# Layer weights cast on the way in by GpSimd's DMAs, eight `zT` buffers, and five more q turned by the crossbar

## The chip, the cores and the metric

The kernel runs on one core of one Trainium2 chip. The metric is the time of one execution on the device in microseconds (us); less is better. Engines are named as in the profile: PE is TensorE's matrix multiplication (PEld its weight loads), DVE is VectorE, ACT is ScalarE, POOL is GpSimd, SP is SyncE, whose queue issues nearly all DMAs.

## The reference, cut to what matters

Attention with a threshold (8 batches, 8 heads, 576 positions, 64 wide), then a layer with a tanh-shrink on the joined heads (4608 tokens, 512 to 2048 to 512). All in float32.

```python
scores = scale * np.matmul(q, k.transpose(0, 1, 3, 2))
thresh = np.max(scores, axis=-1, keepdims=True) - tau
scores = np.where(scores >= thresh, scores, -1000000000.0)
scores = scores - np.max(scores, axis=-1, keepdims=True)
attn = np.exp(scores)
attn = attn / (np.sum(attn, axis=-1, keepdims=True) + 1e-09)
attn_out = np.matmul(attn, v)
x = attn_out.transpose(0, 2, 1, 3).reshape(B * S, H * D)
h = x @ w_in
g = h - np.tanh(h)
out = g @ w_out
```

## The kernel before, in words

The work is 32 pairs of heads, four pairs to a batch. A pair's 1152 score rows make nine tiles of 128 rows, so there are 288 tiles in all. One Python loop over `s` (line 663) writes out the order of all engines by hand: each turn of it is a *slot*, and in slot `s` tile `s + 8` gets its scores, tile `s + 5` its threshold, tile `s` its exponentials, and tile `s - 2` is multiplied with the values. Each engine runs its instructions in the order in which the loop wrote them, and waits for others by semaphores.

What happens to a tile: PE multiplies q with k in two halves (`psS`, lines 303 and 313; q and k are split into a high and a low fp16 part, which lie beside each other in the partitions, and `kS` is k's turned tile with its two halves of partitions swapped). DVE takes the scores out of PSUM with their row maximum (`sc`, line 323) and makes the shift from it (`nb`, line 337). ACT makes the threshold with a steep Prelu (`z`, line 357). The tile is turned, by PE (`psZ`, line 377) for pairs 0 to 3 and part of pairs 4 to 7, else by a crossbar DMA that SP issues (`zT`, line 365). ACT takes the exponentials (`pT`, lines 386 and 394), PE multiplies with the values (`psO`, lines 412 and 423), DVE divides by the sums (`osb`, lines 438 and 443) and, after one more turn on PE, copies the result into the layer's input (`xT`, `xR`).

The inputs of a pair are prepared some slots ahead by a plan (`PREP`, line 621). Where `first` is nine times the pair's number less 8, less 16, 15 and 14 slots from there SP loads k, q and v as float32. In slots `first - 8` and `first - 7` POOL splits k and q, each in three instructions (lines 176, 179, 180; tiles `khl` and `qhl`). In slot `first - 5` PE turns k with nine matrix products, DVE copies it out of PSUM (`kT`, line 250) and POOL copies the swapped halves (`kS`, line 256, two instructions). In slot `first - 4` POOL casts v (lines 208 to 213). q is turned like k in slot `first - 3` (line 227, copied out by DVE at line 250), or, where `q_by_dma(p)` holds, by one crossbar DMA in slot `first - 5` that SP issues and that writes `qT` directly (line 239). The pair's first scores stand in slot `first`.

The layer's work begins in slot 40 for the first stage, and is spread between the attention tiles: PE makes `psH` (line 478), ACT the tanh (`th`, line 491), DVE the difference (`g`, line 497), and PE the second product (`psY`, line 504), one batch behind. After the last tile the rest of the layer runs alone. The product with w_out begins with the second stage, in slot 76.

The layer's weights are two float32 matrices of 4 MB each. `w_pieces` (line 593) cuts each into eight pieces of 128x1024. In every fourth slot, from slot -5 on (`w_when`, line 651), SP loads the next piece into one of two buffers (`wt`, lines 613 and 617), after POOL has cast the piece loaded four slots earlier to bf16 (line 605). `w_load` and `w_cast` hold these two steps:

```python
if s + AHEAD in w_when:
    if loaded:
        w_cast()
    piece = next(pieces, None)
    if piece:
        w_load(piece)
```

Of the kernel before, what the change touches and what calls it, by code (L numbers as in the profile page):

```python
# [9 lines left out]
F32 = mybir.dt.float32  # L10
# [8 lines left out]
def kernel(  # L19
# [11 lines left out]
    nc = tc.nc  # L31
    P = 128
# [13 lines left out]
    HPAIR = H // 2  # L46
# [14 lines left out]
    AHEAD = 8  # L61
# [33 lines left out]
    for i in range(NM):  # L95
# [9 lines left out]
    pool = lambda name, bufs, **kw: ctx.enter_context(  # L105
        tc.tile_pool(name=name, bufs=bufs, **kw)
    )
# [4 lines left out]
    sc_pool = pool("sc", AHEAD - MASK + 2)  # L112
    st_pool = pool("st", 12)
    z_pool = pool("z", 4)
    zt_pool = pool("zt", 6)
    p_pool = pool("p", 3)
    o_pool = pool("o", 2)
    wt_pool = pool("wt", 2)
    g_pool = pool("g", 2)
    t_pool = pool("t", 3)  # L120
    y_pool = pool("y", 2)
# [108 lines left out]

    def q_by_dma(p):

        return p >= 2 * HPAIR and p % 2 == 1

    def turn(p, t):
        hl = hls.pop((p, t))
# [22 lines left out]
    def turn_first(t, part):  # L259

        hl = hls[0, t[0]]
        c0, c1 = ((0, 5), (5, TPP))[part]
        pl, tag = (ps_y, "y") if t == "ks" else (ps_h, "h")
        ps = pl.tile([P, 5 * P], FP16, name=f"ps1_{t}", tag=tag)
        for c in range(c0, c1):
            o = ps[:, (c - c0) * P : (c - c0 + 1) * P]
            if t == "ks":
                for a in range(2):
                    turn_chunk(o[64 * a : 64 * a + 64, :], c, hl[:, c, 1 - a, :])
            else:  # L270
                turn_chunk(o, c, hl[:, c, :, :].rearrange("p a d -> p (a d)"))
        if part == 0:
            mats[0, t] = qk_pool.tile([P, W], FP16, name=f"{t}T", tag=t)
        dst, n = mats[0, t][:, c0 * P : c1 * P], (c1 - c0) * P
        if part == 1 or t == "q":
            nc.scalar.copy(out=dst, in_=ps[:, 0:n])
        else:
            nc.vector.tensor_copy(out=dst, in_=ps[:, 0:n])
# [10 lines left out]
    def scores(i):  # L289
        p, j = divmod(i, TPP)  # L290
        qT, kT, kS = mats[p, "q"], mats[p, "k"], mats[p, "ks"]
        ps = ps_big.tile([P, 1024], F32, name="psS", tag="big")
        main, rem, lo = slice(0, 512), slice(512, 576), 0
        if kind(j) == "B":
            main, rem, lo = slice(512, 1024), slice(448, 512), 448
        if j == 4:
            qrem = REM
            if q_by_dma(p):
                qrem = (slice(512, 640, 2), slice(513, 640, 2))
            for n, kk in enumerate((kT, kS)):  # L300
                for dst, srcs in ((main, MAIN), (rem, REM)):
                    for hh in range(2):
                        nc.tensor.matmul(  # L303
                            out=ps[64 * hh : 64 * hh + 64, dst],
                            lhsT=qT[:, qrem[hh]], rhs=kk[:, srcs[hh]],
                            start=(n == 0), stop=(n == 1),
                        )
        else:
            hh = int(j > 4)
            lhs = qT[:, j * P : (j + 1) * P]  # L310
            for n, kk in enumerate((kT, kS)):
                for dst, src in ((main, MAIN[hh]), (rem, REM[hh])):
                    nc.tensor.matmul(  # L313
                        out=ps[:, dst], lhsT=lhs, rhs=kk[:, src],
                        start=(n == 0), stop=(n == 1),
                    )
        sc = sc_pool.tile([P, S], F32, name="sc")
        if kind(j) == "B":
            mx = mxs[i] = mxs.pop(i - 1)
        else:  # L320
            mx = mxs[i] = st_pool.tile([P, 2], F32, name="mx", tag="mx")
        c = int(kind(j) == "B")
        nc.vector.tensor_scalar(  # L323
            out=sc, in0=ps[:, lo : lo + S], scalar1=SC, scalar2=None,
            op0=ALU.mult, op1=ALU.max, accum_out=mx[:, c : c + 1],
        )
        scs[i] = sc

    def shift(i):

        kd = kind(i % TPP)
        if kd == "A":
            return
        n = 2 if kd == "B" else 1
        mx = mxs.pop(i)
        nb = st_pool.tile([P, 2], F32, name="nb", tag="nb")
        nc.vector.tensor_scalar(  # L337
            out=nb[:, 0:n], in0=mx[:, 0:n], scalar1=-1.0, scalar2=tau,
            op0=ALU.mult, op1=ALU.add,
        )  # L340
        nbs[i] = nb[:, n - 1 : n]
        if kd == "B":
            nbs[i - 1] = nb[:, 0:1]

    def kink(i):
        sc, nb = scs.pop(i), nbs.pop(i)
        kd = kind(i % TPP)
        if kd == "B":
            zt = zs.pop(i - 1)
            z = zt[:, S:W]  # L350
        elif kd == "A":
            zt = zs[i] = z_pool.tile([P, W], BF16, name="z")
            z = zt[:, 0:S]
        else:
            zt = zms[i // TPP % NM]
            z = zt[:, 0:S]
        nc.scalar.activation(  # L357
            out=z, in_=sc, func=ACT.Prelu, bias=nb, scale=1.0, alpha=STEEP
        )
        if on_pe(i):  # L360
            zts[i] = zt
        elif kd != "A":
            n = 5 if kd == "M" else TPP
            zts[i] = zt_pool.tile([P, TPP, P], BF16, name="zT")
            nc.sync.dma_start_transpose(out=zts[i][:, 0:n, :], in_=zt)
# [226 lines left out]

    def w_pieces():
        for w, sb, n in ((moe_w_in, w_in_sb, DM_C), (moe_w_out, w_out_sb, DF_C)):
            flat = sb.rearrange("p c n -> p (c n)")
            cols = n * w.shape[1] // 8
            src = w.rearrange("(c p) n -> p c n", p=P)
            for i in range(8):
                yield flat, src, i, cols, w.shape[1]

    loaded = []

    def w_cast():
        flat, wt, i, cols = loaded.pop(0)
        nc.gpsimd.tensor_copy(out=flat[:, i * cols : (i + 1) * cols], in_=wt)

    def w_load(piece):
        flat, src, i, cols, width = piece
        wt = wt_pool.tile([P, cols], F32, name="wt", tag="wt")
        if cols >= width:  # L610
            r = cols // width
            s = src[:, i * r : (i + 1) * r, :]
            nc.sync.dma_start(out=wt.rearrange("p (c n) -> p c n", n=width), in_=s)
        else:
            r = width // cols
            s = src[:, i // r, (i % r) * cols : (i % r + 1) * cols]
            nc.sync.dma_start(out=wt, in_=s)
        loaded.append((flat, wt, i, cols))


    PREP = (
# [26 lines left out]
    for t in ("k", "q", "v"):  # L648
        load(1, t)
    pieces = w_pieces()  # L650
    w_when = [4 * i + 3 for i in range(17)]

    todo, stage = [], 0
    fold = const.tile([P, 64], BF16, name="fold")
# [8 lines left out]
    for s in range(-AHEAD, NTILE + LAG + 3):  # L663
        p, j = divmod(max(s, 0), TPP)
        if 0 <= s < NTILE and j == 2 + LAG and p % HPAIR == 0 and p >= HPAIR:
            assert not todo
            todo = layers(stage, False)
            share = len(todo) / (HPAIR * TPP - 2 - LAG)
            done, stage = 0.0, stage + 1
        if 0 <= s + AHEAD - 1 < NTILE:  # L670
            shift(s + AHEAD - 1)
        if 0 <= s + AHEAD < NTILE:
            scores(s + AHEAD)
        if s == 1 - AHEAD:
            for t in ("k", "q", "ks"):
                turn_first(t, 1)
        for i in kinks.pop(s, []):
            kink(i)
        bend()
        if 0 <= s < NTILE:  # L680
            weights(s)
            if todo:
                done += share
                if j == TPP - 1 and p % HPAIR == HPAIR - 1:
                    done = 1e9
                while todo and done >= 1:
                    todo.pop(0)()
                    done -= 1
        if s == 0:
            nc.vector.tensor_tensor(  # L690
                out=fold, in0=ident_bf[:, 0:64], in1=ident_bf[:, 64:P], op=ALU.add
            )
        shrink()
        for store in stores[:-1]:
            store()
        del stores[:-1]
        if 0 <= s - LAG < NTILE:
            attend(s - LAG)
            pp, jj = divmod(s - LAG, TPP)
            if jj == 4:  # L700
                norm(pp, 0)
            if jj == 8:
                norm(pp, 1)
        pp, jj = divmod(s - LAG, TPP)
        if jj == 1 and 0 < pp <= NPAIR:
            emit_x(pp - 1)
        for step in plan.pop(s, []):
            step()
        if True:
            if s + AHEAD in w_when:  # L710
                if loaded:
                    w_cast()
                piece = next(pieces, None)
                if piece:
                    w_load(piece)

    while stage < NMB:
        for step in layers(stage, True):
# [44 lines left out]
```

## Time and profile before

| | |
|---|---|
| median of 6 runs | 544.73 us (544.27 to 545.67) |
| profiled execution, its own time | 544.8 us |
| its span in the profile | 542.7 us |
| PE busy | 509.5 us (94%), x4790 |
| DVE busy | 447.3 us (82%), x1196 |
| ACT busy | 439.4 us (81%), x630 |
| POOL busy | 291.0 us (54%), x390 |
| SP's DMA queue, share of 16 engines | 73.6% |
| HBM read, written | 36.70 MB, 9.44 MB |

The shares are means over stages that differ: the attention runs alone at first (to some 70 us), then attention and layer together (to some 470 us), then the layer alone. PE's clock was granted in full throughout. The part of the profiled execution's time that its span does not cover is 2.1 us.

### The profile page before, as it was taken

To read this page: it belongs to the slowest core of one execution; us is meant where nothing else is said; L and a number is where in the kernel's file an instruction comes from. 1 tells how busy PE (TensorE), PEld (TensorE's weight loads), DVE (VectorE), ACT (ScalarE), POOL (GpSimd) and SP (SyncE) were. 2 spreads that over 40 slices of the span, in tenths; PEclk is the share of its full clock that TensorE was granted. 3 is DMA by queue.
4 is the path that set the end of the run, shared out by engine and by line. 5 is a ranking of instruction groups with operands and counts; after the bars stand their busy time and mean duration, and the time that the engine had idled before them with its cause. 6 is when DMAs were issued, how large, how long until landed. Compare 5 with 4: busy or idle time off the path is not lost.

```text
span 542.7 us, 13030 instructions
## 1 busy us (share of the span) xinstructions
PE 509.5 (94%) x4790; PEld 289.1 (53%) x4790; DVE 447.3 (82%) x1196; ACT 439.4 (81%) x630; POOL 291.0 (54%) x390
## 2 busy tenths in 40 slices
PE   4888888888999999999999999999999999899997
PEld 3566655555555455555555555555555555444444
DVE  4999999899888899889988989989989988544440
ACT  4899999998898888889888989899888989633330
POOL 7999987666456666557555755666655730000000
PEclk9999999999999999999999999999999999999999
DMA  6554798668897989799997999999999965310103
GB/s 203 176 184 144 205 203 174 149 137 184 150 176 157 174 171 194 167 185 201 187 191 162 174 201 186 166 175 187 191 180 178 200 127 116 83 41 39 40 39 77
DMA packets 202239, 85.13 MB, mean 157 GB/s; under 512 B 169792, under 2 KB 194624, under 8 KB 202176
## 3 DMA queue, kind: packets, MB, share of 16 engines
q1 hardware_dynamic: 201584, 83.89, 73.6%
q8 instruction: 37, 0.61, 0.5%
q10 hardware_dynamic: 592, 0.43, 0.3%
q14 instruction: 26, 0.21, 0.1%
HBM read 36.70 MB, written 9.44 MB: 85 GB/s over the span
## 4 chain that ended last, share of the span: by engine, by line
PE 68%; DVE 19%; POOL 6%; ACT 3%; issue 2%; DMA 1%; SPq 0%; DVEq 0%; POOLq 0%; ACTq 0%
PE psY L504 20%; PE psH L478 18%; PE psS L313 14%; DVE sc L323 9%; PE psO L423 5%; DVE g L497 3%; PE psS L303 3%; PE ps_k L227 3%; PE psHt L478 3%; DVE nb L337 2%; ACT z L357 1%; DVE osb L438 1%; POOL kS L256 1%; PE psO L412 1%; PE ps_q L227 1%
## 5 line engine op out<-in xcount | busy, mean ns | idle before, releaser
L323 DVE TENSOR_SCALAR_CACHE_REDUCE sc<-psS 128x576 f32<-128x576 f32 x288 | 215.5, 749 | 14.9 <-PE psS L313 10.0
L357 ACT ACTIVATE z<-sc,nb 128x576 bf16<-128x576 f32 x256 | 194.1, 771 | 21.1 <-DVE nb L337 20.4
L504 PE MATMUL psY<-w_out_sb,g 128*128 128x512 bf16 (+1 forms) x592 | 145.8, 374 | 0.0
L256 POOL COPY kS<-kT 64x1152 f16<-64x1152 f16 x62 | 70.9, 1143 | 134.8 <-DVE nb L337 133.2
L394 ACT ACTIVATE pT<-zT 128x1152 f16<-128x1152 bf16 (+1 forms) x128 | 137.3, 1073 | 0.0
L478 PE MATMUL psH<-xT,w_in_sb 128*128 128x512 bf16 x480 | 124.1, 379 | 5.8 <-DVE g L497 4.6
L313 PE MATMUL psS<-kT,qT 128*128 128x512 f16 (+1 forms) x512 | 104.8, 286 | 11.6 <-DVE sc L323 9.6
L491 ACT ACTIVATE th<-psH 128x512 f32<-128x512 f32 x128 | 75.4, 589 | 39.1 <-PE psH L478 38.2
L313 PEld LDWEIGHTS <-qT 128*128 128x128 f16 x1024 | 72.9, 97 | 61.1 <-issue 13.9
L497 DVE SCALAR_TENSOR_TENSOR g<-th,psH 128x512 bf16<-128x512 f32 x128 | 87.2, 682 | 18.4 <-ACT th L491 18.4
L313 PE MATMUL psS<-kS,qT 128*128 128x512 f16 x496 | 101.3, 286 | 0.1
L478 PEld LDWEIGHTS <-w_in_sb 128*128 128x128 bf16 x576 | 49.3, 98 | 60.7 <-issue 7.1
L504 PEld LDWEIGHTS <-g 128*128 128x128 bf16 x592 | 51.0, 98 | 56.6 <-issue 2.9
L423 PEld LDWEIGHTS <-pT 128*128 128x128 f16 x1280 | 55.5, 98 | 25.0 <-issue 1.7
L423 PE MATMUL psO<-vb,pT 128*128 128x65 bf16 x1280 | 61.2, 193 | 0.6 <-ACT pT L394 0.6
L337 DVE TENSOR_SCALAR nb<-mx 128x2 f32<-128x2 f32 (+1 forms) x160 | 49.2, 307 | 2.5
L386 ACT ACTIVATE pT<-psZ 128x640 f16<-128x640 bf16 (+1 forms) x56 | 37.5, 669 | 5.2 <-PE psZ L377 5.0
L180 POOL TENSOR_TENSOR khl<-kraw,khl 128x576 f16<-128x576 f32 x31 | 39.7, 1280 | 2.6
L180 POOL TENSOR_TENSOR qhl<-qraw,qhl 128x576 f16<-128x576 f32 x31 | 39.7, 1280 | 2.6
L250 DVE COPY kT<-ps_k 128x1152 f16<-128x1152 f16 x31 | 23.4, 756 | 13.3 <-PE ps_k L227 12.8
L514 DVE COPY yo<-psY 128x512 f32<-128x512 f32 (+1 forms) x31 | 21.1, 680 | 11.4 <-PE psY L504 6.9
L438 DVE TENSOR_TENSOR osb<-psO,rc 128x256 bf16<-128x256 f32 x64 | 27.2, 425 | 2.2
(77 smaller groups left out, 507.6 us busy)
## 6 DMA issues: line engine op xcount, KB each, us to landing
vraw<-in_v_dram SPq DMA_DIRECT2D x32, 256.0 KB, 3.6
out_dram<-yo SPq DMA_DIRECT2D x32, 256.0 KB, 3.0
kraw<-in_k_dram SPq DMA_DIRECT2D x31, 256.0 KB, 3.2
qraw<-in_q_dram SPq DMA_DIRECT2D x31, 256.0 KB, 3.7
wt<-in_moe_w_in_dram SPq DMA_DIRECT2D x8, 512.0 KB, 5.1
wt<-in_moe_w_out_dram SPq DMA_DIRECT2D x8, 512.0 KB, 4.0
zT<-z SPq DMA_TRANSPOSE x104, 3.6
kraw<-in_k_dram SPq DMA_DIRECT2D x32, 32.0 KB, 2.8
```

Of the source, the lines that this page charges most:

```text
L180: nc.gpsimd.tensor_tensor(out=hl[:, :, 1, :], in0=x, in1=hl[:, :, 0, :], op=ALU.subtract)
L256: nc.gpsimd.tensor_copy(out=o, in_=i)
L313: nc.tensor.matmul(out=ps[:, dst], lhsT=lhs, rhs=kk[:, src], start=(n == 0), stop=(n == 1),)
L323: nc.vector.tensor_scalar(out=sc, in0=ps[:, lo : lo + S], scalar1=SC, scalar2=None, op0=ALU.mult, op1=ALU.max, accum_out=mx[:, c : c + 1],)
L337: nc.vector.tensor_scalar(out=nb[:, 0:n], in0=mx[:, 0:n], scalar1=-1.0, scalar2=tau, op0=ALU.mult, op1=ALU.add,)
L357: nc.scalar.activation(out=z, in_=sc, func=ACT.Prelu, bias=nb, scale=1.0, alpha=STEEP)
L394: nc.scalar.activation(out=pt[:, 0 : n * P], in_=zts.pop(i)[:, 0:n, :], func=ACT.Exp)
L423: nc.tensor.matmul(out=po[:, (j - 1 - 5 * hh) + ab, :], lhsT=pt[:, blk * P : (blk + 1) * P], rhs=vb[:, hh, c, :], start=(n == 0), stop=(n ...
L478: nc.tensor.matmul(out=ps, lhsT=w_in_sb[:, c, n * P : (n + 1) * P], rhs=xs[m][:, c, :] if m < B else xR[:, c, :, :], start=(c == 0), stop= ...
L491: nc.scalar.activation(out=th, in_=ps, func=ACT.Tanh)
L497: nc.vector.scalar_tensor_tensor(out=gs[m][:, n, :], in0=th, scalar=-1.0, in1=ps, op0=ALU.mult, op1=ALU.add,)
L504: nc.tensor.matmul(out=ps, lhsT=gs[m][:, n, ms * P : (ms + 1) * P], rhs=w_out_sb[:, n, cols], start=(n == 0), stop=(n == DF_C - 1),)
```

## The change

Three edits. The casts of the weights on POOL and the loads on SP become one DMA for each piece, issued by POOL, which reads float32 and writes bf16 straight into the weight tiles; the two `wt` buffers are gone. It stands in the slots in which SP loaded the pieces, so four slots ahead of where POOL cast them. The pool of `zT` tiles has eight buffers in place of six. `q_by_dma`, which held for odd pairs from 9 on, now holds for pairs 2, 3, 4, 5 and for odd pairs from 7 on; those five more pairs' q go through the crossbar in slot `first - 5`. Their turns on PE and copies on DVE in slot `first - 3` are gone.

```diff
-    zt_pool = pool("zt", 6)
+    zt_pool = pool("zt", 8)
     p_pool = pool("p", 3)
     o_pool = pool("o", 2)
-    wt_pool = pool("wt", 2)
...
     def q_by_dma(p):
-        return p >= 2 * HPAIR and p % 2 == 1
+        return p in (2, 3, 4, 5) or p > 5 and p % 2 == 1
...
     def w_pieces():
         for w, sb, n in ((moe_w_in, w_in_sb, DM_C), (moe_w_out, w_out_sb, DF_C)):
-            flat = sb.rearrange("p c n -> p (c n)")
-            cols = n * w.shape[1] // 8
             src = w.rearrange("(c p) n -> p c n", p=P)
             for i in range(8):
-                yield flat, src, i, cols, w.shape[1]
-
-    loaded = []
-
-    def w_cast():
-        flat, wt, i, cols = loaded.pop(0)
-        nc.gpsimd.tensor_copy(out=flat[:, i * cols : (i + 1) * cols], in_=wt)
-
-    def w_load(piece):
...
+                if n >= 8:
+                    c = slice(i * n // 8, (i + 1) * n // 8)
+                    yield sb[:, c, :], src[:, c, :]
+                else:
+                    c, cols = i // 2, w.shape[1] // 2
+                    h = slice(i % 2 * cols, (i % 2 + 1) * cols)
+                    yield sb[:, c, h], src[:, c, h]
...
-    w_when = [4 * i + 3 for i in range(17)]
+    w_when = [4 * i + 3 for i in range(16)]
...
-        if True:
-            if s + AHEAD in w_when:
-                if loaded:
-                    w_cast()
-                piece = next(pieces, None)
-                if piece:
-                    w_load(piece)
+        if s + AHEAD in w_when:
+            dst, src = next(pieces)
+            nc.gpsimd.dma_start(out=dst, in_=src)
```

More of the change, by code (lines that the diff above doesn't have):

```diff
@@ L594, in w_pieces @@
         for w, sb, n in ((moe_w_in, w_in_sb, DM_C), (moe_w_out, w_out_sb, DF_C)):
-            flat = sb.rearrange("p c n -> p (c n)")
-            cols = n * w.shape[1] // 8
             src = w.rearrange("(c p) n -> p c n", p=P)
             for i in range(8):
-                yield flat, src, i, cols, w.shape[1]
-    loaded = []
-    def w_cast():
-        flat, wt, i, cols = loaded.pop(0)
-        nc.gpsimd.tensor_copy(out=flat[:, i * cols : (i + 1) * cols], in_=wt)
-    def w_load(piece):
[L608 to L618, printed above, removed]
+                if n >= 8:
[5 more added lines that the diff above has]
+                    yield sb[:, c, h], src[:, c, h]
     PREP = (
```

## The prediction

> **What bounds the kernel now.** I read the slices of the page first, to see where the engines differ over time. Each line is the span in 40 slices of 13.6 us, each digit a busy share in tenths.
>
> ```profile
> DVE  4999999899888899889988989989989988544440
> ACT  4899999998898888889888989899888989633330
> POOL 7999987666456666557555755666655730000000
> ```
>
> POOL is at 9 only in the slices from 13.6 to 68 us. That is the stretch in which the weights are cast, so I asked for busy times there. The columns are the stretch, its length, then busy us and instructions of each engine.
>
> ```profile
> core 0: us, PE busy (x) PEld busy (x) DVE busy (x) ACT busy (x) POOL busy (x), PEclk, DMA share, GB/s
> 10.60:73.20 62.60, 54.32 (x735) 38.44 (x733) 58.83 (x164) 57.58 (x93) 59.33 (x72) 1.00 0.62 174
> sum 57.00, PE 49.88 PEld 35.49 DVE 54.47 ACT 53.90 POOL 53.20; mean PE 9.98 PEld 7.10 DVE 10.89 ACT 10.78 POOL 10.64
> ```
>
> The second line is 10.6 to 73.2 us; the last is the sum over 25 to 82 us. In the first, POOL's 72 instructions leave 3.3 us, some 0.05 us between one and the next: POOL never waits. In the second, ACT is idle for 57.00 - 53.90 = 3.1 us and DVE for 2.5 us. POOL is the bound, with two engines close behind it. The chain of waits says the same: it runs along POOL from 37.3 us and leaves it behind a weight cast (start, length, what).
>
> ```profile
> 68.21 1.28 POOL khl L180
> 69.49 0.65 POOL qraw L176
> 70.14 0.05 issue
> 70.20 0.68 POOL qhl L179
> 70.87 0.07 issue
> 70.95 1.28 POOL qhl L180
> 72.23 0.99 POOL w_out_sb L605
> 73.22 0.47 DVE kT L250
> ```
>
> After that the chain is on DVE and PE to 125 us, and from pair 10 on mostly on PE. The edits touch nothing from pair 8 on except buffers. No order depends on the clock, so what is won or lost before about 110 us should reach the end one for one. The profiled execution took 544.8 us, 2.1 us more than its span of 542.7, and the median of the runs is 544.73; I sum against 544.8.
>
> **The casts that go.** The casts, and the issues that are replaced by POOL's own:
>
> ```profile
> L605 POOL CAST w_in_sb<-wt x8: 1032/1040/1042, 19.8 to 54.5; 128x1024 bf16<-128x1024 f32 x8
> L605 POOL CAST w_out_sb<-wt x8: 1035/1040/1072, 60.9 to 105.8; 128x1024 bf16<-128x1024 f32 x8
> L617 SPq DMA_DIRECT2D wt<-in_moe_w_in_dram x8: 340/442/592, 10.4 to 47.4; - x8
> L613 SPq DMA_DIRECT2D wt<-in_moe_w_out_dram x8: 367/518/541, 53.3 to 93.3; - x8
> ```
>
> Up to the swapped key copies (L256) of pair 6 at 74 us there are 11 casts: 11 x 1.04 = 11.4 us of POOL's unbroken run. The five later ones lie where POOL has idle time again (12 of the 43 us from 82 to 125), beside DVE and PE, and are costed at nothing; were POOL full there too they would be worth 5.2 us. SP loses 16 issues of about 0.48 us; it is not on the chain then, so nothing.
>
> **The issues that come.** Because a piece is now issued where it was loaded, one place ahead of its old cast, 12 issues stand on POOL before pair 6's copies in the order of the changed program, against 11 casts in that of before. No row shows a DMA issued by POOL. Call its cost to POOL c. The lower end is 0, if POOL goes on at once; it can't be less, since an instruction is added. The upper end is 1.34 us, the median issue of a crossbar transpose on SP, the costliest kind here. I take 0.75: the nearest rows are SP's issues of the same pieces, 0.44 and 0.52 us, and the nearest pair of rows for POOL's slowness is its copy of 64x1152 fp16 in 1.143 us against DVE's of 128x1152 in 0.756, a factor of 1.5; 0.48 x 1.5 = 0.73. Then POOL's run changes by 12 x 0.75 - 11.4 = -2.4 us. Break-even for this run alone is c = 0.95. What is queued behind each issue on POOL is the next split or copy, for which PE's turn or the next pair's scores wait.
>
> The Trainium skill has a rule that speaks against the change: "DMA: Bandwidth & Descriptors", in Latency and other measured facts, puts the first byte of a GpSimd DMA at about 1 us, against about 0.6 us from SP or ACT, and lays it to the descriptors that the GpSimd cores emit. If all of that 1 us were POOL's, the run would change by 12 - 11.4 = +0.6 us instead. No run here shows yet which holds.
>
> **The q turns.** Pairs 2, 3, 4, 5 and also 7 (odd and over 5) change; pair 7 was below the old limit of 8. Each loses nine PE transposes (0.5 us) and one DVE copy (0.75 us alone, 0.67 in a row of others), and gives SP a transpose. For 2 to 5 the DVE and PE time lies beside POOL's run and is no gain by itself, but DVE's idle time grows from 2.5 by 4 x 0.67 to 5.2 us, so that ACT is the next bound, not DVE. Without this part the early gain would be capped at 2.5 us. For pair 7 the copy is on the chain:
>
> ```profile
> 90.98 0.60 DVE g L497
> 91.58 0.67 DVE qT L250
> 92.25 0.09 DVE nb L337
> ```
>
> So 0.67 us goes; behind it the `nb` and ACT's `z` come earlier. I count 0.7.
>
> The transpose has to land before the pair's first scores. Its rows are those of the twelve pairs turned so far, and for pair 2 the place is seen on POOL and PE:
>
> ```profile
> DMA to landing us min/median/max: 3.3/3.9/5.0
> ```
>
> ```profile
> 25.07 1.28 POOL L180 TENSOR_TENSOR qhl<-qraw,qhl 128x576 f16<-128x576 f32 x1
> 29.27 0.41 PE L313 MATMUL psS<-kT,qT 128*128 128x512 f16 x2
> ```
>
> The split of pair 2 ends at 26.35. Two issues in place of one cast make that 26.35 + 1.5 - 1.04 = 26.8, and 3.9 us later is 30.7: 1.4 us after PE's 29.27 (0.8 and 2.5 with the ends of the landing row). Pair 3: 38.55 + 5 x 0.75 - 4 x 1.04 = 38.1, landed 42.0, needed at 42.77. Pair 4: 49.78 + 7 x 0.75 - 6 x 1.04 = 48.8, landed 52.7, needed at 53.36. Pairs 5 and 7 have more room. So only pair 2 is late, by 1.4 us, and PE's next transposes for ACT stand behind it. Behind the transpose on SP stand the value loads of the next pair, wanted ten slots later, and in pairs 5 and 7 the `zT` turns, of which SP issues one in 1.3 us and the next ones are some five us apart; nothing.
>
> **Early stage, sum.** POOL allows -2.4. ACT allows its 3.1 idle us less the 1.4 of pair 2: -1.7. The smaller gain holds: -1.7. With pair 7's 0.7 that is -2.4, so 544.8 - 2.4 = 542.4 us.
>
> **Without a price.** Eight `zT` buffers: five tiles are turned in nine slots, five slots ahead of their use, so at most three are in flight, and six were enough. The eight later issues wait for issues eight places earlier, 32 slots before. The weights: last piece of w_in issued at slot 23, first read at 40; of w_out at 55, first read at 76. With 4 to 5 us of landing now (1.2 us a slot) three times that would still do. DVE's `nb` (160 of 143 ns at the least, 1276 at the most) is long where a POOL instruction runs; fewer casts can only shorten it, and what it gives is within ACT's idle time.
>
> The same skill, in "SBUF — State Buffer", SBUF: two separate sides, says that descriptors made on GpSimd can't be written while DVE holds the shared port. By the rows DVE's likely holders are the `nb`, 0.17 us at the median; by that rule c could grow by as much now and then.
>
> **Rivals.** *A, slower: the issue costs POOL more than the cast did.* Decides from c = (11.4 + 0.7)/12 = 1.01, and is over the 0.2% (1.1 us) that a measurement of this kernel can tell from no change from c = 1.10. At the upper end, 1.34, POOL's run is 16.1 - 11.4 = +4.7, less 0.7: 548.8 us. For it: POOL is full, the lines above say so, and an issue more than before stands ahead of pair 1's copies, which end at 18.50, 0.5 us before PE reads them. Against: SP's issues of the same pieces, at 0.48, take a third of that.
>
> *B, no change: c between 0.9 and 1.05.* POOL stays the bound, -0.6 to +1.2, less 0.7: 543.5 to 545.3, say 544.4.
>
> *C, more than forecast: c near 0.* Pair 2 is then in time (25.3 + 3.9 = 29.2), the full 3.1 and 0.7 are won: 541.0 us.
>
> *D, slower by the DMA side.* The DMA share is 0.62 in the POOL stretch and at most 0.92. A q turn adds between nothing and 3.9 of 11.2 us (all engines throughout), 0.35. If casting packets took twice as long as the plain ones, the loads of all kinds, 0.62, would at most double. Then landings grow, and one us on each of four q turns past their need is +4: about 548. Against: 0.62 + 0.17 leaves room.
>
> **How the numbers follow.** The forecast (c from 0.4 to 0.9, 541.7 to 543.5) 0.38; C 0.12; B 0.20; A 0.24; D 0.06. Faster by over 0.2%: forecast and C, 0.50. Same: B, 0.20. Slower: A and D, 0.30. The range runs from just under C, 540.8, to just under A's end, 548.2; the likeliest case's own is 541.7 to 543.5.
>
> **What would show it.** Right: no cast on POOL; issue instructions of POOL under 0.9 us; kS of pair 6 at some 72 us instead of 74.1; POOL with real idle time before 73 us and ACT nearly none; first scores of pair 2 waiting about a us for the qT transpose; no qT copy near 91 us; the windows from 125 us on the same length as before. Wrong: POOL still without gaps to 73 us or beyond (A or B, by its length); waits of PE for qT in pairs 3 to 5, or landings over 6 us (D).

## The result, and the profile after

| | before | after |
|---|---|---|
| median | 544.76 us (544.14 to 546.20, 41 runs) | 547.63 us (544.92 to 552.52, 20 runs) |
| ratio, 95% interval | | 1.0051 [1.004, 1.0063] |
| profiled execution, its span | 544.8, 542.7 us | 546.7, 544.9 us |

The change made the kernel slower by about 2.8 us; 542.4 was forecast. The time lies in the forecast's range, but on the wrong side of no change. The runs of after also spread over 7.6 us, those of before over 2.1.

The slices first, as for before: busy tenths, 13.6 us each, with the granted TensorE clock below.

```profile
PE   5878789897999999999999999999999999899996
DVE  4969879899898898899988989989989988544440
ACT  4889989998898888889898989899988989633330
POOL 7979867756466665557555756666655730000000
PEclk9989999999999999999999999999999999999999
```

POOL has gaps from the third slice on, where it had none before the sixth. PE falls to 7 in the third, fifth and tenth slice, where it had 8, and in the third the clock is no longer full. Next the busy times in the stretches of the forecast:

```profile
core 0: us, PE busy (x) PEld busy (x) DVE busy (x) ACT busy (x) POOL busy (x), PEclk, DMA share, GB/s
10.60:73.20 62.60, 51.15 (x666) 35.47 (x663) 52.55 (x156) 53.98 (x88) 54.88 (x72) 0.97 0.74 141
25.00:82.00 57.00, 45.96 (x611) 32.48 (x608) 46.06 (x140) 50.70 (x82) 46.19 (x62) 0.97 0.81 151
```

The forecast said that ACT would lose nearly all of its idle time. In 25 to 82 us it has 57.00 - 50.70 = 6.3 us of it, twice the 3.1 of before, and POOL has 10.8. No engine is the bound here any more; all of them wait for something. POOL's own DMA issues are not to blame:

```profile
L695 POOL DMA_DIRECT2D w_in_sb<-in_moe_w_in_dram x8: 531/608/770, 15.2 to 52.8; - x8
L695 POOL DMA_DIRECT2D w_out_sb<-in_moe_w_out_dram x8: 716/754/799, 54.6 to 95.2; - x8
```

(The attention's and the layer's lines stand one lower in the changed kernel: its L312 is L313 of before.) An issue holds POOL for 0.61 or 0.75 us at the median, against 1.04 for a cast. The waits in 10 to 75 us say what is late (total, times, longest):

```profile
DVE sc L322 <- PE psS L312: 8.4, 9, 3.1
PEld L312 <- DMA qT<-qhl: 7.2, 3, 3.3
ACT pT L385 <- PE psZ L376: 5.3, 5, 1.9
PE psS L312 <- DMA qT<-qhl: 5.3, 2, 3.1
POOL kS L255 <- DVE nb L336: 4.0, 2, 3.3
```

PE waits three times for a q turn: 3.09 us for pair 2 (to 31.7), 1.33 for pair 4 (to 54.4) and 2.24 for pair 5 (to 67.8), 6.7 us in all. (PE's own line has two of them; the line of its weight loads, PEld, has all three. The 8.4 us of the first line are DVE waiting for the scores, mostly behind the same waits.) Here is PE around the first of them:

```profile
28.24 0.39 PE L376 MATMUL psZ<-ident_bf,z 128*128 128x128 bf16 x4
31.71 0.42 PE L312 MATMUL psS<-kT,qT 128*128 128x512 f16 x2 [3.09 <-DMA qT<-qhl]
31.97 0.64 PE L312 MATMUL psS<-kS,qT 128*128 128x512 f16 x2
32.42 0.72 PE L376 MATMUL psZ<-ident_bf,z 128*128 128x128 bf16 x5
```

Compare the durations: the same products took 0.42 us in the second row and 0.64 in the third. The windows by the clock say why (clock granted: third figure from the end):

```profile
25.00:32.00 7.00, 3.87 (x52) 2.67 (x49) 4.50 (x15) 6.28 (x11) 6.65 (x10) 1.00 0.73 134
32.00:35.40 3.40, 3.40 (x30) 2.29 (x29) 1.99 (x5) 1.59 (x3) 3.22 (x5) 0.50 1.12 246
35.40:73.00 37.60, 31.57 (x452) 22.73 (x451) 33.30 (x104) 34.83 (x57) 31.72 (x42) 1.00 0.79 141
```

The first two stretches in before:

```profile
25.00:32.00 7.00, 6.41 (x90) 4.60 (x87) 6.79 (x21) 7.00 (x13) 6.64 (x8) 1.00 0.42 130
32.00:35.40 3.40, 3.38 (x60) 2.59 (x58) 3.33 (x11) 3.40 (x7) 3.25 (x5) 1.00 0.63 218
```

For 3.4 us right behind the wait PE ran at half its clock: 30 products in that stretch, where before had 60 in its own 32 to 35.4 us. The forecast had no such term. (The DMA share, second from the end, counts a packet's whole time where the packet starts; so it can pass 1 in a short stretch.)

And POOL, whose run was to be shorter, but unbroken:

```profile
35.60 1.30 POOL L179 TENSOR_TENSOR qhl<-qraw,qhl 128x576 f16<-128x576 f32 x1
40.18 2.33 POOL L255 COPY kS<-kT 64x1152 f16<-64x1152 f16 x2 [3.28 <-DVE nb L336]
```

`kS` of pair 3 reads `kT`, which DVE copies at 39.29 in after and at 35.67 in before, because PE turns that k late, behind its wait. (The row names `nb`, DVE's next instruction behind that copy.) So POOL stands idle for 3.28 us, all that follows it moves, the split of pair 4 among it, and pair 4's turn is late too.

How the delay runs can be read from the first `sc` of each pair, counted from that of pair 0 (which stands at 9.65 us in before and at 8.63 in after):

| first `sc` of pair | 1 | 2 | 3 | 4 | 5 | 6 | 7 | 8 | 11 |
|---|---|---|---|---|---|---|---|---|---|
| before, us | 10.2 | 20.7 | 33.6 | 44.7 | 57.0 | 70.5 | 85.1 | 99.8 | 144.6 |
| after, us | 11.3 | 24.1 | 35.4 | 46.6 | 60.0 | 74.3 | 88.0 | 102.7 | 147.5 |

After loses 3.4 us by pair 2, wins half of it back by pair 3, loses again in pairs 5 and 6, and keeps 2.9 us to the end. Not all of the 3.4 belongs to the wait: 1.2 of it stands at pair 1 already, before any q turn is waited for, and the casting DMAs alone (`e1_casts` below) are 1.0 us late there too, and win 1.0 back by pair 3.

### The profile page after: what moved, and what is told of

Same layout as the page of the kernel before. It is cut to its first block, busy times and chain, and to the rows that moved or that the text cites. A ratio compares the mean times of both kernels' runs of the same rounds, so it can differ in the third digit from the quotient of the medians.

```text
span 544.9 us, 12925 instructions
## 1 busy us (share of the span) xinstructions
PE 509.4 (93%) x4745; PEld 287.9 (53%) x4745; DVE 441.0 (81%) x1191; ACT 438.9 (81%) x630; POOL 284.8 (52%) x390
## 4 chain that ended last, share of the span: by engine, by line
PE 68%; DVE 16%; POOL 5%; DMA 4%; ACT 3%; issue 2%; SPq 1%; ACTq 0%; DVEq 0%; POOLq 0%
PE psY L503 19%; PE psH L477 17%; PE psS L312 15%; DVE sc L322 8%; PE psO L422 5%; DVE g L496 3%; PE psS L302 3%; PE psHt L477 3%; PE ps_k L226 3%; DMA vraw<-in_v_dram 2%; DVE nb L336 2%; DMA qT<-qhl 1%; PE ps_q L226 1%; PE psO L411 1%; DVE osb L437 1%
## 5 line engine op out<-in xcount | busy, mean ns | idle before, releaser
L312 PE MATMUL psS<-kT,qT 128*128 128x512 f16 (+1 forms) x512 | 105.7, 288 | 14.8 <-DVE sc L322 7.3
L312 PEld LDWEIGHTS <-qT 128*128 128x128 f16 x1024 | 73.0, 98 | 64.9 <-issue 11.8
L312 PE MATMUL psS<-kS,qT 128*128 128x512 f16 x496 | 101.9, 287 | 0.0
L336 DVE TENSOR_SCALAR nb<-mx 128x2 f32<-128x2 f32 (+1 forms) x160 | 45.3, 283 | 2.7
```

The lines of the kernel that those rows point to most:

```text
L312: nc.tensor.matmul(out=ps[:, dst], lhsT=lhs, rhs=kk[:, src], start=(n == 0), stop=(n == 1),)
L336: nc.vector.tensor_scalar(out=nb[:, 0:n], in0=mx[:, 0:n], scalar1=-1.0, scalar2=tau, op0=ALU.mult, op1=ALU.add,)
```

## The experiments

My theory after the result: the casting DMAs bring their gain, and the crossbar turns of pairs 2 to 5 take it back and more, because PE waits for them. The rivals: the DMA traffic as such costs the time (in whichever part); the eight buffers or pair 7 do; POOL's issues do.

### One part alone

`e1_casts`: the changed kernel, q as before.

```diff
-        return p in (2, 3, 4, 5) or p > 5 and p % 2 == 1
+        return p >= 2 * HPAIR and p % 2 == 1
```

> The changed kernel with q turned as before (crossbar for odd pairs from 9 on): the casting DMAs and the eight zT buffers alone. Theory L (late turns: PE is held until the crossbar has landed qT of pairs 2, 4 and 5, 6.7 us of waits in the changed kernel's trace): 12 issues (eight of 0.61 and four of 0.75 us) stand for 11 casts, POOL's run is 11.4 - 7.9 = 3.5 us shorter, capped by ACT's 3.1 idle us: 541.6 to 543.0 us, no wait of PE for qT before 115 us. Theory T (traffic: the added transposes and casting packets lengthen all landings, waits for qT are one symptom): 543 to 544.5. Theory C (the casting DMAs themselves cost): over 545.5.

Measured: ratio 0.9968 [0.9957, 0.9979], 544.16 us beside 545.59. (Every ratio here is taken against runs of before made beside it, whose median lay between 544.6 and 545.7 us; so ratios compare, medians less well.) The casting DMAs, with the eight buffers, are a gain of about 1.7 us: on 544.8 that is 543.1, at the border between theories L and T. PE waits for no q turn before 115 us, as L has it.

`e2_q`: the kernel before, with the new line of `q_by_dma` alone.

> The kernel before with only the new choice of pairs for the crossbar; weights still loaded by SP and cast by POOL, six zT buffers. Theory L: with 4 to 4.5 us of landing pair 2 is 1.2 to 1.6 us late, pair 3 up to 0.3, pair 4 0.5 to 0.9, less 0.7 for pair 7: 545.5 to 547.5 us, with PE waiting for qT in pairs 2 and 4. Theory T: the traffic is about that of the changed kernel, so also 546 to 548, and landings of loads grow by a us or more. Theory C: 544 to 545, since no casting DMA is there.

Measured: 1.0106 [1.0092, 1.0121], 551.09 us, more than any of the theories allowed. The q turns alone cost more than the whole change. The waits in 10 to 75 us:

```profile
PE psS L313 <- DMA qT<-qhl: 6.7, 4, 3.1
POOL w_in_sb L605 <- DMA wt<-in_moe_w_in_dram: 6.3, 2, 4.0
PE ps_k L227 <- POOL khl L180: 3.8, 1, 3.8
```

The first is the wait for the turn. The second belongs to SP's queue: the turn waits there for POOL's split, and the loads of weights stand behind it, so that POOL's casts wait for them, and PE for POOL. The casting DMAs of the full change take the weights out of that queue. That may be why both edits together cost 0.51%, and not the 1.06 - 0.32 = 0.74% of their sum; it was not tried by itself.

### Traffic or waiting

`e3_aside`: the casting DMAs; the same five turns go through the crossbar, into a tile that nobody reads, and PE turns q as before.

```diff
+        nc.sync.dma_start_transpose(
+            out=m.rearrange("p (c r) -> p c r", c=TPP),
+            in_=hl.rearrange("p c a d -> p (c a d)"),
+        )
...
+        if p in (2, 3, 4, 5, 7):
+            plan.setdefault(first - 5, []).append(lambda p=p: turn_aside(p))
```

> As the casting DMAs alone, with the same five crossbar turns of q (pairs 2, 3, 4, 5, 7) issued in the same slots into a tile that nothing reads, while PE and DVE turn q for use as before: the traffic without the wait. Theory L: within 0.5 us of the casting DMAs alone, 541.8 to 543.5. Theory T: near the changed kernel, 546.5 to 548.

Measured: 0.9991 [0.998, 1.0002], 544.99 us. All the traffic without anybody waiting for it costs 0.23% over the casts alone, about 1.3 us. The full change costs 0.83% over them. So most of the loss is in the waiting, as theory L has it, though the traffic costs more than the 0.5 us that L allowed.

`e4_pair7`: the changed kernel, with pairs 2 to 5 turned by PE; `e8_pair67` has pairs 6 and 7 by the crossbar, `e9_only2` of pairs 2 to 5 only pair 2, `e10_pairs34` only 3 and 4 (the last two with pair 7).

```diff
-        return p in (2, 3, 4, 5) or p > 5 and p % 2 == 1
+        return p > 5 and p % 2 == 1                       # e4_pair7
+        return p in (6, 7) or p > 7 and p % 2 == 1        # e8_pair67
+        return p == 2 or p > 5 and p % 2 == 1             # e9_only2
+        return p in (3, 4) or p > 5 and p % 2 == 1        # e10_pairs34
```

> The changed kernel with pairs 2 to 5 turned by PE as before and pair 7 still by the crossbar. Theory L: 0.3 to 0.7 us under the casting DMAs alone (the DVE copy of 0.67 us at 91 us leaves the chain; pair 7 has 5 us of room), 541.0 to 542.5. Theory T: at or above the casting DMAs alone. Theory C: over 545.

> As with pair 7 alone, and pair 6 through the crossbar too. Pair 6's qT copy by DVE lies at 77 us in the chain of before, 0.67 us. POOL's run ends there, and pair 6's split ends some 5 us before its first scores. Theory L: 0 to 0.7 us less than with pair 7 alone, 541.5 to 543, if it lands within 5 us; if it lands later, each us late is a us lost, 543 to 545. Theory T: 0.2 to 0.5 us more than with pair 7 alone.

> The changed kernel with, of pairs 2 to 5, pair 2 alone through the crossbar (and pair 7 and the odd pairs above, as in the changed kernel). Theory F (one first late turn breaks POOL's run, and pairs 4 and 5 are late only because POOL then runs behind): PE waits about 3 us for pair 2's qT, POOL stands idle some 3 us before pair 3's key copies, and most of the 1.0% between the changed kernel and pair 7 alone is there: 545.5 to 547.5 us. Theory S (each late turn costs its own wait): 3.1 of 6.7 us of waits, 544 to 545.5.

> The changed kernel with, of pairs 2 to 5, pairs 3 and 4 alone through the crossbar: the two whose turns landed after 3.2 and 3.9 us. Theory F: with no stall at pair 2 both land before their first scores, PE waits under 1 us for qT, and the time is that of pair 7 alone: 541.5 to 543.5. Theory S: pair 4 keeps its 1.3 us, 543 to 544.5. Theory T (the traffic): 0.5 us or more over pair 7 alone of the same call.

| pairs by the crossbar, of 2 to 7 | ratio, 95% interval | median us |
|---|---|---|
| none (`e1_casts`) | 0.9968 [0.9957, 0.9979] | 544.16 |
| 7 (`e4_pair7`) | 0.9951 [0.9936, 0.9966] | 542.69 |
| 6, 7 (`e8_pair67`) | 0.9979 [0.9969, 0.9990] | 543.57 |
| 3, 4, 7 (`e10_pairs34`) | 0.9962 [0.9945, 0.9978] | 544.73 |
| 2, 7 (`e9_only2`) | 1.0079 [1.0050, 1.0108] | 548.97 |
| 2, 3, 4, 5, 7 (after) | 1.0051 [1.0040, 1.0063] | 547.63 |

(The ratio of `e10_pairs34` leaves out two of its nine runs, 550.4 and 550.6 us at a mean clock of 0.993, the lowest of its clocks; the median has them.) Pairs 3 and 4 cost nothing that the other seven show, pair 2 alone costs as much as all of them and more than either theory of its run allowed: 1.0079 is 549.1 on 544.8. Pair 6 costs 0.28% over pair 7 alone by these rows, more than was expected, but a repeat of pair 7 alone (below) is too far from its first figure to call that an effect. PE in `e9_only2`:

```profile
27.57 0.39 PE L376 MATMUL psZ<-ident_bf,z 128*128 128x128 bf16 x4
33.14 0.66 PE L312 MATMUL psS<-kT,qT 128*128 128x512 f16 x2 [5.18 <-DMA qT<-qhl]
```

and its POOL, where the same copies as in after stand idle, now for 4.65 us:

```profile
41.47 2.32 POOL L255 COPY kS<-kT 64x1152 f16<-64x1152 f16 x2 [4.65 <-DVE nb L336]
```

### Can the turn be made in time?

`e5_apart`: the pieces are issued two at a time at other slots, so that none stands just ahead of a q turn. `e6_apart7`: the same, with only pair 7 by the crossbar.

```diff
-    w_when = [4 * i + 3 for i in range(16)]
+    w_when = [9 * (i // 2) + (6, 8)[i % 2] for i in range(16)]
```

> The changed kernel with the sixteen weight pieces issued by POOL two at a time after a pair's value cast, never between a split and the turn that waits for it. In the changed kernel the q turns of pairs 2 and 5 were issued 0.1 us behind a piece and landed after 5.6 and 6.9 us, those of pairs 3, 4 and 7, with no piece beside them, after 3.2, 3.9 and 4.0. Theory P (the pieces beside the turns make them late): landings of 3.2 to 4.2 us, waits of PE for qT under 3.5 us in place of 6.7, 543.5 to 545.5 us. Theory L (the turns are late by their place, 2 to 3 us after the split, whatever lies beside them): waits stay over 5 us, 546 to 548.

> Casting DMAs, crossbar for pair 7 and the odd pairs above, pairs 2 to 5 by PE, and the pieces placed as in the run with the pieces apart. Nothing waits for a q turn here before pair 7, so theories P and L both say: as with pair 7 alone (0.9951 of before), and up to 0.5 us less, because no issue stands ahead of pair 1's and pair 2's key copies: 542 to 543 us. If it is slower by over 0.5 us, two issues in a row cost more than two apart.

Measured: 0.9998 [0.9976, 1.0020] and 0.9974 [0.9964, 0.9983]. Moving the pieces takes back some 0.5% of the change's loss, though in its profile the waits are hardly shorter (3.17, 0.97 and 1.83 us) and the turns of pairs 2 and 5 land after 5.1 and 6.5 us instead of 5.6 and 6.9. So the time is that of theory P and the waits, 6.0 us in all, are those of theory L: neither holds. The runs spread from 541.3 to 547.5 and go with the clock: three at a mean clock of 0.999 or 1.0 took 541.3 to 542.2 us, nine at 0.993 to 0.997 took 544.2 to 547.5, while no run of after stands over 0.997. So the gain may lie in the clock; that is not shown. `e6_apart7` is 0.23% slower than `e4_pair7`, over the 0.5 us that would speak against two issues in a row, but again the repeat of the latter leaves that open.

`e7_qfirst`: q of pairs 2 to 5 is split before k, so that the turn starts earlier.

```diff
-        (8, lambda p: split(p, "k")),
-        (7, lambda p: split(p, "q")),
+        (8, lambda p: split(p, "q" if p in (2, 3, 4, 5) else "k")),
+        (7, lambda p: split(p, "k" if p in (2, 3, 4, 5) else "q")),
```

> The changed kernel with q of pairs 2 to 5 split by POOL before k instead of after: the q turn can start 2.6 us sooner, k's split ends 2.6 us later. Theory L: the waits for qT of 3.1, 1.3 and 2.2 us fall to at most 0.5 us in all; what is late next is k's turn on PE, for which the three slots between the k and the q turn of before are the room: 542.5 to 545. Theory T (the traffic itself costs): 546 to 548, though the turns land in time.

Measured: 1.0090 [1.0057, 1.0123], 549.25 us. PE no longer waits for a q turn; it waits for the key split instead, in each of the four pairs:

```profile
PE ps_k L226 <- POOL khl L179: 7.2, 4, 2.0
```

The two orders of the split choose which wait stands there. These waits are not all of the loss: the profiled run, the slowest of the seven at 553.0 us, loses 5.6 us more by the first scores of pair 8, where ACT waits 3.69 us for a `zT` turn that landed after 8.2, PE waits 4.25 us for ACT, and the clock is halved from 104.1 to 110.9 us (and from 63.1 to 66.6 behind the last of the four waits).

### The smaller parts

`e11_pair7_zt6` and `e12_pair7_again` ran on one chip: casting DMAs and pair 7, with six and with eight `zT` buffers (the second is `e4_pair7` once more).

```diff
-    zt_pool = pool("zt", 8)
+    zt_pool = pool("zt", 6)                               # e11_pair7_zt6
```

> Casting DMAs, pair 7 through the crossbar, and six zT buffers in place of eight. By the count of at most three tiles in flight the buffers do nothing: within 0.3% of the same kernel with eight, in the same call. If six are too few, 1 us or more above it.

> The kernel with the casting DMAs and pair 7 again, on the same chip as the other three of this call, as their base: 0.994 to 0.998 of before, 541.7 to 544 us.

Measured: 0.9962 [0.9948, 0.9976] with six, 1.0005 [0.9980, 1.0029] with eight. Eight show no gain. And the same kernel gave 0.9951 on one chip and 1.0005 on another, so that pair 7's own effect, 0.67 us by the forecast, is below what these runs can tell. In `e12_pair7_again` the times go with the clock: four runs at a mean clock of 0.992 to 0.994 took 547.1 to 549.5 us, the eight at 0.996 and over 542.8 to 546.5.

### The half clock

Theory: the stretch at half clock that follows PE's idle time costs time of its own. Rival: it only lies beside the wait. To tell them apart PE gets products that nobody reads, just where it waited. The score tile that they write is written anew by the real scores, and the output is untouched.

```diff
+        if j == 0:
+            for _ in range({2: 12, 4: 5, 5: 8}.get(p, 0)):      # e14_fill
+            # {2: 18} in e16_only2_fill
+                nc.tensor.matmul(
+                    out=ps[:, 0:512], lhsT=mats[p - 1, "q"][:, 0:P],
+                    rhs=mats[p - 1, "k"][:, 0:512], start=True, stop=True,
+                )
```

`e13_after_again` (the changed kernel) and `e15_only2_again` (`e9_only2` once more) are the partners on the same chip.

> The changed kernel as it is, the partner on the same chip of the next run. Both theories: 1.004 to 1.007 of the kernel before (546.5 to 548.5 us), runs spread over 3 us or more, mean granted clock .985 to .997, some run with a stretch of half clock after the first scores of pair 2.

> The changed kernel, and TensorE is given products that nobody reads just ahead of the first scores of pairs 2, 4 and 5 (12, 5 and 8 of 128x128x512, 0.22 us each: 2.6, 1.1 and 1.8 us), where it waited 3.1, 1.3 and 2.2 us for the q turn. The output is not touched by them: the same tile is written anew by the scores. Theory half clock costs: the stretch of 3.4 us at half rate after the wait goes, the mean granted clock is .997 or more, and the time falls by 1 to 2 us against the run beside it, to 545 to 546.5, with less spread. Theory only the wait costs: the clock may rise, the time stays within 0.5 us of the run beside it or grows by up to 1 us where a turn lands sooner than the extra products end.

> Of pairs 2 to 5 only pair 2 is turned by the crossbar; the same kernel as before under this description, as the partner on this chip of the next run. Both theories: 1.005 to 1.010 of the kernel before, one TensorE wait of about 5 us that ends near 33 us, and a stretch at half clock after it.

> As the run beside it (only pair 2 of 2 to 5 by the crossbar), with 18 products that nobody reads (3.9 us) ahead of pair 2's first scores, where TensorE waited 5.2 us. The output is not touched by them. Theory half clock costs: no stretch at half rate near 33 us, time 1 to 2 us below the run beside it. Theory only the wait costs: the same time within 0.5 us, at whatever clock.

| | ratio, 95% interval | median us | mean clock of its runs |
|---|---|---|---|
| before | 1 | 544.65 | 12 runs 0.999 or 1.0, 6 runs 0.997 |
| `e13_after_again` | 1.0065 [1.0041, 1.0090] | 547.69 | 0.989 to 0.995 |
| `e14_fill` | 1.0020 [0.9996, 1.0044] | 545.47 | 7 runs 0.999 or 1.0, 5 runs 0.991 to 0.997 |
| `e15_only2_again` | 1.0076 [1.0057, 1.0095] | 548.30 | 0.989 to 0.997 |
| `e16_only2_fill` | 1.0033 [1.0020, 1.0045] | 546.02 | 0.999 or 1.0 |

Adding work that nobody uses made both kernels faster, by 2.2 and 2.3 us. (For the first pair the two intervals just touch, for the second they are apart.) The turn of pair 2 is no earlier in `e16_only2_fill`: it landed 5.7 us after its issue at 26.1, in its partner 5.8 us after 26.2. Its rows show the idle stretch full, and the products behind it at full rate:

```profile
28.29 0.39 PE L382 MATMUL psZ<-ident_bf,z 128*128 128x128 bf16 x4
28.70 4.04 PE L295 MATMUL psS<-kT,qT 128*128 128x512 f16 x18
32.59 0.41 PE L318 MATMUL psS<-kT,qT 128*128 128x512 f16 x2
32.83 0.41 PE L318 MATMUL psS<-kS,qT 128*128 128x512 f16 x2
```

and its window beside that of its partner, `e15_only2_again`, where PE waited 3.24 us to 32.1:

```profile
32.00:35.40 3.40, 3.40 (x48) 2.34 (x47) 1.96 (x7) 1.85 (x4) 3.21 (x5) 1.00 1.11 289
```

```profile
32.00:35.40 3.40, 3.33 (x28) 2.23 (x29) 1.39 (x5) 1.37 (x2) 3.22 (x5) 0.52 1.12 284
```

In the same 3.4 us, 48 products (four of them the last of the added ones) against 28. In `e14_fill` the cover did not always hold: its profiled run (546.92 us) still waited 1.98 us for pair 2's turn, and a half-clock stretch follows: the turn landed after 7.1 us, later than the 12 products could cover. Its seven runs at full clock took 543.8 to 545.7 us, the other five 545.6 to 550.7. The theory that the half clock has its own cost holds; the size is a little over the 1 to 2 us expected.

## Why the prediction was wrong, point by point

**The cost c of an issue on POOL: right.** 0.75 was taken, 0.61 and 0.75 were measured, so rivals A (from 1.01) and C (near 0) fall. The Trainium skill, in "DMA: Bandwidth & Descriptors", Latency and other measured facts, puts the first byte of a GpSimd DMA at about 1 us; that all of it would be POOL's time, as the forecast weighed it, does not agree with these rows. The casts alone bring 1.7 us (`e1_casts`), where POOL's run allowed 2.4 and DVE 2.5. One reading behind that sum was uneven: POOL's 3.3 us of idle time were read in 10.6 to 73.2 us, ACT's 3.1 and DVE's 2.5 in 25 to 82, where POOL has 57.00 - 53.20 = 3.8 us; it was not the fullest of the three there. In the profile of `e1_casts` POOL has 7.8 us of idle time in 25 to 82 us, DVE 4.2 and ACT still 3.0; but that profiled run took 544.6 us, 0.2 less than that of before, so it does not show the gain, and what limits it stays open.

**The landing of the q turns: the step that failed.** "So only pair 2 is late, by 1.4 us" (PE then waited 3.09 us for pair 2, 1.33 for pair 4 and 2.24 for pair 5) rested on a landing of 3.9 us from turns that all start after 117 us. In this stage they took 5.6, 3.2, 3.9 and 6.9 us for pairs 2 to 5, up to 7.1 for pair 2 in `e9_only2`. The upper end of that row, 5.0, was stated, and even it was too low. The DMA share that I used to dismiss rival D was a mean over 62 us; in 25 to 32 us, about the turn of pair 2, it is 0.73, where before had 0.42, and in 29 to 32 us it is 1.15. The queues in 26 to 31.7 us of after, from pair 2's turn to its landing (packets, MB, share of 16 engines):

```profile
q1 hardware_dynamic: 1490, 0.55, 47.2%
q0 software_dynamic: 144, 0.26, 35.2%
```

q0 carries the casting pieces. It holds the DMA engines for a third of that time, for a third of the bytes. But a casting piece just ahead is not the whole cause: `e2_q` has none, and its turns of pairs 2 and 3 land after 5.1 us, as the turn of pair 2 does in `e5_apart`. What else makes the landing long, the input loads that SP issues right behind the turn for one, was not tried.

**What a late turn costs: under-sized twice.** I charged 1.4 us once, against ACT's idle time. But PE's wait holds back the next key turn, that holds back `kS`, and POOL, on which the gain rested, stood idle for 3.28 us; so the split of pair 4 ended at 50.44 (51.5 by the count of before, whose first scores come 1.0 us later) instead of the forecast's 48.8, and pair 4 was late without a long landing. And the half clock behind the wait, a term that the sum did not have, is worth 2.2 us by `e14_fill`, whose added products covered the wait in part of its runs only.

**The sum as the runs give it.** Casting DMAs with the eight buffers -1.7 us (`e1_casts`). The q turns of pairs 2 to 5 and 7: 1.0051 - 0.9968 = 0.83%, +4.5 us; of it some 2.2 the half clock, and the other 2.3 the waits and the traffic. Together +2.8.

**Pair 7 and the buffers.** The 0.67 us of pair 7 could not be told; that eight `zT` buffers change nothing for the better agrees with what was measured. That nothing comes of the `zT` turns behind pair 7's q turn on SP is doubtful: in the profiles of `e10_pairs34` and `e7_qfirst` ACT waits 2.08 and 3.69 us, up to 98 and 103.5 us, for a `zT` turn issued behind it, though not in that of after, and no run sets this apart.

**The rivals.** D came nearest: landings over 6 us, turns past their need, 548 us. It had 0.06, argued down by a mean share. It did not have the clock either.

## What to carry to other kernels

When a transfer takes the place of work on an engine, take its latency from the stage in which it will run, with its queues, and put the upper end on whichever engine waits; if that engine feeds the one on which the gain rests, the loss is paid there again. On TensorE a wait of some microseconds can cost more than its length: look at the clock behind it too. Two edits that come together deserve a run each: here one of them gains 0.3% and the other loses more than that.

The better version is the change without the turns of pairs 2 to 5: 0.9951 to 0.9968 in `e4_pair7`, `e11_pair7_zt6` and `e1_casts`, though a repeat of the first gave 1.0005.

## What the runs showed of the hardware

**TensorE's clock halves behind an idle stretch.** The granted clock drops to 0.50 for one or two stretches of 3.4 us, most of them beginning between 0.8 us before a wait's end and 0.4 us behind it: in after (wait of 3.09 us), `e13_after_again` (3.08, two stretches), `e14_fill` (1.98), `e15_only2_again` (3.24), `e9_only2` (5.18), `e5_apart` (3.17), `e7_qfirst` (1.94, and two more stretches from inside a wait of 4.25) and `e2_q` (3.84, but not behind its 3.13). Four others (`e3_aside`, `e6_apart7`, `e8_pair67`, `e10_pairs34`) have one at 122 to 131 us, 1.2 to 2.1 us after waits of 1.45 to 1.75 for pair 9's turn; the other profiles have waits of 1.0 to 1.8 us there too and kept the full clock, before (1.47) and `e4_pair7` (1.74) among them. So the length of the wait alone does not decide. `e10_pairs34` there (the window of the wait, and the next):

```profile
124.00:127.10 3.10, 1.35 (x22) 0.90 (x20) 3.03 (x8) 2.88 (x4) 2.95 (x4) 1.00 0.73 149
127.10:130.60 3.50, 3.50 (x18) 1.15 (x15) 2.68 (x8) 3.27 (x6) 0.68 (x1) 0.51 0.93 136
```

What decides can be read from the 18 profiles. In each, the stretches at full and at half clock are whole multiples of 3.41 us up to the kernel's end (20.48 is 6 of them, 112.64 is 33), so the time can be cut into windows of that length. Of some 2770 such windows at full clock, the next one was halved behind all ten in which PE was busy for 1.52 us or less, behind three of ten with 1.66 or 1.67 us, and behind none with more. The limit lies near half a window. That is why the 3.13 us of `e2_q` cost no clock: they fell into two windows, in each of which PE was still busy for 1.75 us.

The Trainium skill states this in "TensorE: Matmul & The Clock Gate", Part 1: the clock is halved after an idle window of about 3.4 us, and the windows run freely, so that the same kernel varies from run to run. The 3.4 us stretches and the spread agree with it. But a window without any work was not needed: in the first row above PE was busy for 1.35 of 3.1 us, and the clock was halved all the same.

The kernel also starts at the slow rate: before 10.0 us the profile of before records no granted clock, and the pairs of products that take 0.41 us later take 0.66 there. Its clock was full from then on, not throughout.

**The runs spread with the clock.** One such stretch lowers a run's mean clock by 0.5 x 3.4 / 543 = 0.003; 6 of the 18 runs of before beside `e14_fill` stand at 0.997. In `e14_fill`, one kernel on one chip, runs at a mean clock of 0.999 or 1.0 have a median of 544.0 us, those below 546.9.

**A DMA issued by POOL** of 128x1024 float32 to bf16 held POOL for 0.53 to 0.80 us and landed after 3.5 to 6.2 us.
